# Five chunks of up to 496 tokens in place of eight of 288 in a feed-forward stage, with its weights in six groups

## The chip, the cores and the metric

The kernel runs on one core of a Trainium2 chip. The metric is the device time of one execution in microseconds; the times below are medians of several executions. The core has a matrix engine (TensorE, PE in the profile; its weight loads are PEld), VectorE (DVE), ScalarE (ACT) and GpSimd (POOL), which run side by side and wait for each other by semaphores, and 16 DMA engines, whose queue is fed here by SyncE (SP). Operands lie in SBUF, 128 partitions wide; TensorE writes to PSUM, which has eight banks of 512 f32 columns.

## The reference, cut to what matters

Three layers follow each other, on 4 x 576 = 2304 tokens of 512 features. The second one is the stage that is changed: 2048 hidden features, in 16 blocks of 128.

```python
def reference(q, k, v, s, U, V, w_ch1, w_ch2, w_gate, wq, wk, wv, wo):
    x = attention(q, k, v, s)            # causal, with a bias from cumulated gates; 4 x 8 heads of 64
    u = x + (U @ V mixed over the tokens of a batch)(x)
    x = u + np.maximum(u @ w_ch1, 0.0) @ w_ch2       # feed-forward, 512 -> 2048 -> 512
    return gated_attention_experts(x, w_gate, wq, wk, wv, wo)   # 4 experts, the best two of each token
```

The result has to be that of f32. TensorE is used in a faster mode with fewer bits of the operands, so each f32 operand a is split into a high part ah and the rest al, and a product is made of three: ah bh + ah bl + al bh. The weights arrive as 64-bit floats and are turned into f32 on the chip.

## The kernel before

**Stages.** The program has three stages. In the first (0 to 309 us) the 32 heads of attention run, and in their gaps the mixing of batches 0 to 2 and the first three hidden blocks (FA = 3) of these batches, whose results go to DRAM (aD). The second (309 to 673 us) is the feed-forward stage with the other 13 blocks, L790 to L916. The third holds the experts' attention and the output.

**Tiling of the feed-forward stage.** The tokens lie along the columns, and a chunk has CH = 288 of them, so there are eight chunks. The 13 blocks are taken in groups, `GROUPS = [2, 3, 3, 3, 2]`. A group goes over all chunks, every second group backwards, so that the chunk at a turn is used twice; this list of pairs (group, chunk) is `items`. In group 0 the chunks of the last batch (two of the eight) are preceded by the first three blocks on them, since the first stage did not do these. The unit of work is a slot, one block f on one chunk c. In it `ffn1` (L818) issues 12 matmuls (four pieces of 128 features, three products each) into one of three PSUM banks, from the parts uh and ul of the chunk and the block's weights; ScalarE then writes hh, the high part of the result after relu (L830), and VectorE hl, the low part (L831). `ffn2` (L837) of a pair (f, c) comes two slots later (`len(pend) > 2`): 12 matmuls into four accumulators (facc), 128 output features each. After the last block of a group VectorE adds the four accumulators to aT, in the last group to uT (L851).

**What runs beside it.** Each slot also issues background work, after its matmuls:
- `uprep` makes uh and ul of the next chunk out of uT (`u_split`, L273): four copies on ScalarE (uh, L277) and four subtractions (ul, L278), the first on VectorE, the other three on GpSimd (ULF = "vggg"). In a group of three blocks two of the four come in each of the first two slots, in a group of two all four in the first slot. Two sets of tiles (`fua`, `fub`) take turns.
- `conv` makes the weights of the next group: four pieces of 256 columns to a block. A piece is loaded (c_raw), ScalarE squares it (c_mk, L106), VectorE takes six instructions (L109, L113, L118, L122, L127, L131), ScalarE writes wh (L198) and GpSimd wl (L201). The steps of neighbouring pieces are interleaved (PLAIN), and they are spread over the slots of a group from the third on: at slot sl so many are issued that (issued) x (nsl - 3) is no less than (sl - 3) x nconv.
- `wp_tasks` loads and splits the weights of the last stage (wpr to WPh on ScalarE and WPl on VectorE, L766), eight pieces, one step at each chunk from the second chunk of group 2 on.
- `mixq`, in group 0, is the mixing of the last batch, two tasks to a slot; its row blocks are split into xh and xl (L241).
- `g_x2` splits the first batch for the last stage (XH, XL) in the last slots.

**What sets the order.** This stage and the one before are issued in the order in which the program writes them, engine by engine (`manual_schedule`, closed at L918): what stands behind a waiting instruction on the same engine waits too. After that line a scheduler orders the last stage. The lines that the change touches or the steps of the prediction use are CH and GROUPS (L27, L47), `u_split`, `ffn_tasks`, `uprep`, `ffn1`, `ffn2`, the loop over `items` from L868, and the pools of weights (`w01p`, `wts`), of u and of the last stage's x2 and y.

## Time and profile before

| | us |
|---|---|
| median of 3 executions (lowest, highest) | 876.32 (875.93, 877.03) |
| the profiled execution | 875.31 |
| its span in the trace | 873.1 |
| TensorE busy in the span | 817.1 (94%) |
| VectorE busy | 602.3 (69%) |
| ScalarE busy | 467.6 (54%) |
| GpSimd busy | 308.1 (35%) |

The span reaches from the first instruction to the last of one execution; the execution's own time has 2.2 us more, and it lies 1.0 us under the median. TensorE's mean granted clock over the span is 0.988 of the full one. The trace names each instruction by engine, line and tile; a busy time is the union of its durations. A matmul's duration reaches from its start to its modelled end and so overlaps the next one; what a row of matmuls takes is read from their starts. The idle time before an instruction is put down to the event that ended it.

### The profile page before, as it was taken

The page shows a single profiled execution, that of the slowest core. Times are in us where ns is not written, and L with a number is a line of the kernel's source. Part 1 is how long each engine was busy: PE and PEld are TensorE (multiplying, and loading weights), DVE is VectorE, ACT ScalarE, POOL GpSimd, SP SyncE. Part 2 cuts the span into 40 slices and gives each one's busy share as a digit, 9 for nine tenths or more (in the row PEclk, how much of TensorE's full clock was granted, in tenths as well). Part 3 has the DMA queues.
Part 4 walks back from the last instruction along what each step waited for, and adds up shares of the span by engine and source line. Part 5 has one row for each costly group of instructions (what it writes and reads, how often), then busy time and mean ns, then how long its engine had stood idle before and what let it go on. Part 6 is the DMA issues. An engine that isn't in the chain of part 4 may idle for free.

```text
span 873.1 us, 17681 instructions
## 1 busy us (share of the span) xinstructions
PE 817.1 (94%) x6104; PEld 750.8 (86%) x6104; DVE 602.3 (69%) x1755; ACT 467.6 (54%) x1382; POOL 308.1 (35%) x458
## 2 busy tenths in 40 slices
PE   3787888999999999999999999999999999999998
PEld 3665676898987789999999999999999989899875
DVE  7787888877787249986875887576546675656541
ACT  6686678866677343323432443333243476566673
POOL 4445254544344224322432432232233033221241
PEclk9997899999999999999999999999999999999999
DMA  7888568787560151120121221121000121211221
GB/s 205 227 230 201 135 179 230 176 208 202 151 180 17 55 187 37 50 61 25 50 53 34 61 61 42 46 62 38 1 1 2 41 43 30 64 46 38 60 69 55
DMA packets 36945, 79.66 MB, mean 91 GB/s; under 512 B 4792, under 2 KB 7992, under 8 KB 36856
## 3 DMA queue, kind: packets, MB, share of 16 engines
q1 hardware_dynamic: 36856, 78.53, 33.8%
q8 instruction: 49, 0.80, 0.4%
q14 instruction: 40, 0.33, 0.1%
HBM read 38.80 MB, written 8.40 MB: 54 GB/s over the span
## 4 chain that ended last, share of the span: by engine, by line
PE 74%; DVE 11%; ACT 5%; DMA 4%; issue 4%; POOL 1%; SPq 1%; DVEq 0%; ACTq 0%; POOLq 0%
PE facc L844 17%; PE hps L826 17%; PE pv L432 9%; PE qkp L1034 6%; PE t L403 4%; PE vps L971 3%; PE ops L1057 3%; PE facc L308 3%; PE qk L362 3%; PE qk L363 3%; PE hps L294 2%; PE t L406 2%; DVE P L373 2%; DMA c_raw_w<-in_w_dram 1%; ACT P L380 1%
## 5 line engine op out<-in xcount | busy, mean ns | idle before, releaser
L278 POOL TENSOR_TENSOR ul<-uT,uh 128x288 fp32r<-128x288 f32 x126 | 103.6, 840 | 176.1 <-ACT uh L277 161.4
L380 ACT ACTIVATE P<-P,stat 64x64 f32<-64x64 f32 (+4 forms) x240 | 133.8, 558 | 46.4 <-DVE stat L373 42.8
L373 DVE CUSTOM_DVE_ANT_0 P<-qk,mask 64x64 f32<-64x64 f32 (+4 forms) x240 | 116.6, 487 | 46.3 <-PE qk L363 30.2
L391 POOL TENSOR_SCALAR P<-P,stat 64x64 f32<-64x64 f32 (+4 forms) x160 | 101.5, 648 | 133.0 <-DVE stat L386 87.2
L362 PE MATMUL qk<-R,L 128*128 128x288 f32 (+4 forms) x288 | 96.6, 340 | 23.1 <-DVE L L573 10.9
L830 ACT ACTIVATE hh<-hps 128x288 fp32r<-128x288 f32 x110 | 44.8, 407 | 135.5 <-PE hps L826 135.4
L844 PE MATMUL facc<-hh,wh 128*128 128x288 f32 x376 | 111.4, 296 | 0.7 <-DVE aT L851 0.7
L76 ACT ACTIVATE pt<-t 64x64 f32<-64x64 f32 (+5 forms) x304 | 89.8, 335 | 41.5 <-PE t L406 35.3
L826 PE MATMUL hps<-ul,wh 128*128 128x288 f32 x376 | 111.3, 296 | 0.0
L826 PE MATMUL hps<-uh,wl 128*128 128x288 f32 x376 | 111.3, 296 | 0.0
L826 PE MATMUL hps<-uh,wh 128*128 128x288 f32 x376 | 111.1, 295 | 0.0
L844 PE MATMUL facc<-hh,wl 128*128 128x288 f32 x376 | 111.0, 295 | 0.0
L844 PE MATMUL facc<-hl,wh 128*128 128x288 f32 x376 | 110.9, 295 | 0.0
L831 DVE SCALAR_TENSOR_TENSOR hl<-hps,hh 128x288 fp32r<-128x288 f32 x110 | 50.1, 456 | 87.6 <-ACT hh L830 87.3
L403 PE MATMUL t<-ident,P 128*128 128x128 f32 x480 | 89.4, 285 | 16.1 <-ACT pt L76 5.3
L391 POOL TENSOR_SCALAR P<-P,stat,pt 64x64 f32<-64x64 f32 (+4 forms) x80 | 48.2, 615 | 127.8 <-DVE stat L386 35.6
L363 PE MATMUL qk<-R,L 68*128 68x288 f32 (+9 forms) x288 | 89.6, 316 | 1.2 <-DMA L<-Cd 0.8
L362 PEld LDWEIGHTS qk<-R,L 128*128 128x128 f32 x288 | 57.5, 200 | 31.5 <-issue 15.0
L403 PEld LDWEIGHTS t<-ident,P 128*128 128x128 f32 x480 | 58.6, 143 | 29.5 <-issue 16.9
L432 PE MATMUL pv<-pt,V 128*64 128x288 f32 (+4 forms) x768 | 79.2, 355 | 0.5 <-DVE stat L373 0.3
L432 PEld LDWEIGHTS pv<-pt,V 128*64 128x64 f32 x768 | 52.5, 144 | 27.5 <-issue 7.0
L201 POOL TENSOR_TENSOR wl<-c_a_w,wh 128x256 fp32r<-128x256 f32 x56 | 43.3, 774 | 91.3 <-ACT wh L198 88.7
(177 smaller groups left out, 2204.3 us busy)
## 6 DMA issues: line engine op xcount, KB each, us to landing
c_raw_w<-in_w_dram SPq DMA_DIRECT2D x64, 256.0 KB
uT<-in_qk_dram SPq DMA_DIRECT2D x15, 576.0 KB
L<-HI SPq DMA_DIRECT2D x28, 288.0 KB
R<-HI SPq DMA_DIRECT2D x28, 288.0 KB
V<-in_v_dram SPq DMA_DIRECT2D x16, 320.0 KB
R<-uT SPq DMA_DIRECT2D x14, 288.0 KB
L<-uT SPq DMA_DIRECT2D x14, 288.0 KB
aD<-stage SPq DMA_DIRECT2D x6, 576.0 KB
```

The source lines that it names most:

```text
L76: nc.scalar.activation(out=out, in_=in_, func=AF.Copy)
L278: eng.tensor_tensor(out=l_, in0=src, in1=h_.bitcast(F32), op=OP.subtract)
L362: nc.tensor.matmul(ps[:, bk, :w], lhsT=q1[:, rows], rhs=k1[:, c0:c0 + w], start=True, stop=False)
L363: nc.tensor.matmul(ps[:, bk, :w], lhsT=q2[:, rows], rhs=k2[:, c0:c0 + w], start=False, stop=True)
L373: nc.vector.tensor_tensor_reduce(out=po, in0=view, in1=mk, scale=-1.0, scalar=3.0e38, op0=OP.add, op1=OP.min, accum_out=stat[P - M:, 0, t: ...
L380: nc.scalar.activation(out=po, in_=po, func=AF.Exp, scale=-1.0, bias=stat[P - M:, 0, t:t + 1], accum_out=stat[P - M:, 1, t:t + 1])
L391: nc.gpsimd.tensor_scalar(out=pv, in0=pv, scalar1=stat[r0:, 2, t:t + 1], scalar2=1.0 if gate is None else gate(t)[r0:], op0=OP.mult, op1=O ...
L403: nc.tensor.transpose(ps[:, P * kb:P * kb + P], Pn[:, c0:c0 + P], ident)
L432: nc.tensor.matmul(ps[64 * hh:64 * hh + 64, half, lo - a:e - a], lhsT=V(hh)[:, kb, :], rhs=pt[:, PST * kb + lo:PST * kb + e], start=kb == ...
L826: nc.tensor.matmul(ps, lhsT=w[:, 0, cs], rhs=x, start=i == 0, stop=i == 11)
L844: nc.tensor.matmul(accs[c][d], lhsT=w[:, 1, cs], rhs=x, start=f == fs[0] and i == 0, stop=f == fs[-1] and i == 2)
L1034: nc.tensor.matmul(ps[:, :HALF], lhsT=wsl(w, "qk", k, col, col + P), rhs=xx[:, c0:c0 + HALF], start=i == 0, stop=i == 11)
```

## The change

- Chunks: four of CW = 496 tokens and one of 320 (CN, C0) in place of eight of 288, in the second stage alone. CH stays for the work that the first stage does.
- Groups: [2, 2, 3, 2, 2, 2] in place of [2, 3, 3, 3, 2]; the groups with index 1 and 3 go backwards (BACK). Where two groups follow each other in the same direction, 4 and 5 behind 3 among them, u of the first chunk is made again.
- The first three blocks in group 0 take only tokens of the last batch (`first_of`): 256 columns of the fourth chunk and the whole fifth.
- Memory: a single tile, `keep`, is allocated once. It holds the weights of the first three blocks and later of groups 2 and 4 (`w_keep`), one set of u (`u_keep`) and the hidden parts in the first stage, and in the last stage x2 (XS), y (ys) and two operands (l1s). The other set of u is the tile `ub`. The weights of groups 1, 3 and 5 come from a pool of two (`w_pool`).
- Background: the four parts of u come two to a slot in every group; mixing comes up to four tasks to a slot, two behind the first product and two behind the second; conversions are spread from the second slot on (nsl - 2 in place of nsl - 3); the weights of the last stage are split from the second chunk of group 1 on, in place of group 2; x2 of the first batch is split in the last two chunks.

```diff
 CH = 288
-NCH = TOK // CH
+CW = 496
+CN = [CW, CW, CW, CW, TOK - 4 * CW]
+C0 = [0, CW, 2 * CW, 3 * CW, 4 * CW]
+NCH = len(CN)
...
-GROUPS = [2, 3, 3, 3, 2]
+GROUPS = [2, 2, 3, 2, 2, 2]
+BACK = (1, 3)
...
-                    Wh[f] = wpool().tile([P, 2, DM], F32R, tag="wh", name=f"wh_{f}")
-                    Wl[f] = wpool().tile([P, 2, DM], F32R, tag="wl", name=f"wl_{f}")
+                    Wh[f], Wl[f] = place(f)
...
+    keep = ctx.enter_context(tc.tile_pool(name="keep", bufs=1, side="right")).tile([P, FA * 4 * DM + 14 * CH], F32R,
+                                                                                name="keep")
+    UB = FA * 4 * DM
+
+    def w_keep(f):
+        i = (f if f < FA else f - FA - sum(GROUPS[:2]) if f < FA + sum(GROUPS[:3]) else f - FA - sum(GROUPS[:4]))
+        return (keep[:, (2 * i + x) * 2 * DM:(2 * i + x + 1) * 2 * DM].rearrange("p (x c) -> p x c", x=2)
+                for x in range(2))
...
+    def u_keep(k, w):
+        return (keep[:, UB + (2 * k + x) * w:UB + (2 * k + x + 1) * w] for x in range(2))
...
+    XS = {0: [keep[:, x * KD * S:(x + 1) * KD * S].rearrange("p (k j) -> p k j", k=KD) for x in range(2)]}
+    ys = [[keep[:, UB + (2 * pr + x) * S:UB + (2 * pr + x + 1) * S] for x in range(2)] for pr in range(2)]
+    l1s = [keep[:, c:c + 2 * S + 64] for c in (2 * KD * S, UB + 4 * S)]
...
-        wts = [cx.enter_context(tc.tile_pool(name="f_w0", bufs=3))]
+        w0 = cx.enter_context(tc.tile_pool(name="f_w0", bufs=2))
...
-        fub = cx.enter_context(tc.tile_pool(name="f_u", bufs=1))
+        ub = cx.enter_context(tc.tile_pool(name="f_u", bufs=1)).tile([P, 8, CW], F32R, name="ub")
...
-        fu = [fua, fub]
+        fu = [u_keep, lambda k, w: (ub[:, 2 * k + x, :] for x in range(2))]
...
+        def w_pool(f):
+            return [w0.tile([P, 2, DM], F32R, tag=f"w{n}", name=f"w{n}_{f}") for n in "hl"]
+
+        def first_of(fs, c):
+
+            return max(0, TOK - S - C0[c]) if fs[0] < FA else 0
...
-                if gi == 2 and l[0][1] != c and not WP:
                     mxs.close()
-                    w01.close()
-                    fus.close()
-                    fu[fu.index(fua)] = cx.enter_context(tc.tile_pool(name="f_u2", bufs=1))
                     wpp = wg.enter_context(tc.tile_pool(name="wpp", bufs=1, side="right"))
...
-                    ffn1(f, c, hi, lo)
+                    ffn1(f, c, hi, lo, first_of(fs, c))
+                    for _ in range(2):
+                        if mixq:
+                            mixq.pop(0)()
                     pend.append((f, c, fs))
                     if len(pend) > 2:
                         ffn2(*pend.pop(0))
+                    for _ in range(2):
+                        if mixq:
+                            mixq.pop(0)()
...
-                    for _ in range(2 if len(fs) > 2 else KD):
+                    for _ in range(2):
                         if uq:
                             uq.pop(0)()
...
-                    if gi == len(items) - 1 and c >= NCH - 3 and len(x2.get(0, "  ")[0]) < KD:
+                    if gi == len(items) - 1 and c >= NCH - 2 and len(x2.get(0, "  ")[0]) < KD:
                         g_x2(0, len(x2[0][0]) if 0 in x2 else 0)
-                    while conv and (nconv - len(conv)) * (nsl - 3) < (sl - 3) * nconv:
+                    while conv and (nconv - len(conv)) * (nsl - 2) < (sl - 2) * nconv:
                         conv.pop(0)()
```

On VectorE, in group 1 before, while three blocks are converted (c_h, c_a, c_z are steps of a piece, hl_1_7 is the low part of block 7 on chunk 1, aT the sums, the first row here the last of four):

```order
L851 TENSOR_TENSOR aT_4003<-facc_5_2_3_5910,aT_4003 128x288
L113 TENSOR_SCALAR c_a_w10_256_6020<-c_h_w10_256_5973 128x256
L118 SCALAR_TENSOR_TENSOR c_a_w10_256_6020<-c_h_w10_256_5973,c_a_w10_256_6020 128x256
L122 TENSOR_SCALAR c_z_w10_256_6023<-c_a_w10_256_6020 128x256
L127 SCALAR_TENSOR_TENSOR c_h_w10_256_5973<-c_raw_w10_256_5886,c_z_w10_256_6023 128x256
L131 TENSOR_TENSOR c_a_w10_256_6020<-c_h_w10_256_5973,c_a_w10_256_6020 128x256
L831 SCALAR_TENSOR_TENSOR hl_1_7_6045<-hps_1_7_6031,hh_1_7_6044 128x288
L109 SCALAR_TENSOR_TENSOR c_h_w10_512_6064<-c_mk_w10_512_6025,c_raw_w10_512_5971 128x256
L113 TENSOR_SCALAR c_a_w10_512_6068<-c_h_w10_512_6064 128x256
L831 SCALAR_TENSOR_TENSOR hl_0_5_6084<-hps_0_5_6070,hh_0_5_6083 128x288
```

And in group 1 of the change, where three blocks are converted too, behind the four sums of the short chunk (WPl is a piece of the last stage's weights):

```order
L880 TENSOR_TENSOR aT_3907<-facc_5_4_3_4787,aT_3907 128x320
L122 SCALAR_TENSOR_TENSOR c_a_w7_256_4827<-c_h_w7_256_4823,c_a_w7_256_4827 128x256
L126 TENSOR_SCALAR c_z_w7_256_4867<-c_a_w7_256_4827 128x256
L131 SCALAR_TENSOR_TENSOR c_h_w7_256_4823<-c_raw_w7_256_4808,c_z_w7_256_4867 128x256
L135 TENSOR_TENSOR c_a_w7_256_4827<-c_h_w7_256_4823,c_a_w7_256_4827 128x256
L113 SCALAR_TENSOR_TENSOR c_h_w7_512_4875<-c_mk_w7_512_4869,c_raw_w7_512_4821 128x256
L117 TENSOR_SCALAR c_a_w7_512_4879<-c_h_w7_512_4875 128x256
L122 SCALAR_TENSOR_TENSOR c_a_w7_512_4879<-c_h_w7_512_4875,c_a_w7_512_4879 128x256
L126 TENSOR_SCALAR c_z_w7_512_4882<-c_a_w7_512_4879 128x256
L131 SCALAR_TENSOR_TENSOR c_h_w7_512_4875<-c_raw_w7_512_4821,c_z_w7_512_4882 128x256
L135 TENSOR_TENSOR c_a_w7_512_4879<-c_h_w7_512_4875,c_a_w7_512_4879 128x256
L780 TENSOR_TENSOR WPl_4764<-wpr_0_4765,WPh_4763 128x514
```

Where five conversion instructions stood between the sums and hl_1_7 and two before hl_0_5, ten and a WPl now stand between the sums and hl_2_5, the next row.

On ScalarE, in the same group before (hh_1_6 is the high part of block 6 on chunk 1, uh_0_2 a part of chunk 0, which is the next one, wh a piece of new weights, c_mk the square):

```order
L830 ACTIVATE hh_1_5_5945<-hps_1_5_5932 128x288
L277 ACTIVATE uh_0_0_5961<-uT_68 128x288
L277 ACTIVATE uh_0_1_5965<-uT_68 128x288
L198 ACTIVATE wh_10_5975<-c_a_w10_0_5925 128x256
L830 ACTIVATE hh_1_6_5992<-hps_1_6_5979 128x288
L277 ACTIVATE uh_0_2_6012<-uT_68 128x288
L277 ACTIVATE uh_0_3_6016<-uT_68 128x288
L106 ACTIVATE c_mk_w10_512_6025<-c_raw_w10_512_5971 128x256
L830 ACTIVATE hh_1_7_6044<-hps_1_7_6031 128x288
L198 ACTIVATE wh_10_5975<-c_a_w10_256_6020 128x256
```

And in the change (`ub` and `keep` hold u and the new weights; x2 stands for two copies):

```order
L857 ACTIVATE hh_2_5_4905<-hps_2_5_4892 128x496
L286 ACTIVATE ub_3920<-uT_68 128x496 x2
L201 ACTIVATE keep_74<-c_a_w7_512_4879 128x256
L110 ACTIVATE c_mk_w8_0_4938<-c_raw_w8_0_4888 128x256
L201 ACTIVATE keep_74<-c_a_w7_768_4933 128x256
L857 ACTIVATE hh_2_6_4964<-hps_2_6_4951 128x496
L286 ACTIVATE ub_3920<-uT_68 128x496 x2
L110 ACTIVATE c_mk_w8_256_4990<-c_raw_w8_256_4942 128x256
L201 ACTIVATE keep_74<-c_a_w8_0_4948 128x256
```

The second pair of u copies, which was followed by a whole slot of block 7 before the next chunk began, is now issued in the chunk's last slot, behind two pieces wh of the weights that wait for VectorE.

## Rows read from the trace of the kernel before

**Rows 1.** the page: busy time, share of the span, instructions, by engine:
```profile
PE 817.1 (94%) x6104; PEld 750.8 (86%) x6104; DVE 602.3 (69%) x1755; ACT 467.6 (54%) x1382; POOL 308.1 (35%) x458
```

**Rows 2.** stretches: length; busy us of PE, PEld, DVE, ACT, POOL; clock; DMA:
```profile
309.00:364.00 55.00, 52.34 (x382) 50.34 (x383) 44.28 (x99) 22.33 (x60) 19.74 (x24) 1.00 0.31 104
350.00:360.00 10.00, 8.83 (x67) 8.60 (x65) 9.60 (x22) 3.83 (x11) 4.20 (x5) 1.00 0.16 50
404.00:481.00 77.00, 77.00 (x582) 77.00 (x581) 57.41 (x137) 28.83 (x79) 26.08 (x34) 1.00 0.18 46
```

**Rows 3.** TensorE's timeline around 500 us: start, duration, line, operation, out<-in, shapes:
```profile
500.45 0.30 PE L826 MATMUL hps<-uh,wh 128*128 128x288 f32 x1
...
502.97 0.29 PE L844 MATMUL facc<-hl,wh 128*128 128x288 f32 x1
```

**Rows 4.** TensorE's timeline near the end of the program:
```profile
864.05 0.39 PE L1057 MATMUL ops<-WPh,yh 128*128 128x512 f32 x1
...
868.64 0.40 PE L1057 MATMUL ops<-WPh,yl 128*64 128x512 f32 x1
```

**Rows 5.** VectorE's timeline, 420 to 425 us:
```profile
420.62 1.06 DVE L118 SCALAR_TENSOR_TENSOR c_a_w<-c_h_w,c_a_w 128x256 uint32<-128x256 uint32 x1
...
422.04 0.43 DVE L127 SCALAR_TENSOR_TENSOR c_h_w<-c_raw_w,c_z_w 128x256 f32<-128x256 uint32 x1
...
422.99 0.46 DVE L831 SCALAR_TENSOR_TENSOR hl<-hps,hh 128x288 fp32r<-128x288 f32 x1
423.36 1.54 DVE L851 TENSOR_TENSOR aT<-facc,aT 128x288 f32<-128x288 f32 x4
```

**Rows 6.** VectorE by line, 328-361 us: count, busy, mean ns, idle before:
```profile
L127 DVE SCALAR_TENSOR_TENSOR c_h_w<-c_raw_w,c_z_w 128x256 f32<-128x256 uint32 x6 | 3.5, 587 | 0.2
L122 DVE TENSOR_SCALAR c_z_w<-c_a_w 128x256 uint32<-128x256 uint32 x6 | 3.4, 561 | 0.2
L118 DVE SCALAR_TENSOR_TENSOR c_a_w<-c_h_w,c_a_w 128x256 uint32<-128x256 uint32 x5 | 3.2, 640 | 0.1
L113 DVE TENSOR_SCALAR c_a_w<-c_h_w 128x256 uint32<-128x256 uint32 x5 | 2.6, 512 | 0.2
L109 DVE SCALAR_TENSOR_TENSOR c_h_w<-c_mk_w,c_raw_w 128x256 f32<-128x256 f32 x6 | 2.6, 426 | 0.4
L131 DVE TENSOR_TENSOR c_a_w<-c_h_w,c_a_w 128x256 f32<-128x256 f32 x6 | 2.5, 423 | 0.2
```

**Rows 7.** GpSimd's timeline, with the idle time before and what ended it:
```profile
420.59 0.81 POOL L278 TENSOR_TENSOR ul<-uT,uh 128x288 fp32r<-128x288 f32 x1 [1.13 <-ACT uh L277]
```

**Rows 8.** VectorE by line and shape, 364 to 672 us:
```profile
L851 DVE TENSOR_TENSOR aT<-facc,aT 128x288 f32<-128x288 f32 x104 | 40.1, 448 | 0.0
...
L278 DVE TENSOR_TENSOR ul<-uT,uh 128x288 fp32r<-128x288 f32 x29 | 13.6, 467 | 0.0
...
L766 DVE TENSOR_TENSOR WPl<-wpr,WPh 128x514 fp32r<-128x514 f32 x8 | 5.8, 721 | 5.5 <-ACT WPh L765 5.5
```

**Rows 9.** VectorE by line and shape, 300 to 364 us:
```profile
L241 DVE TENSOR_TENSOR xl<-mx,xh 128x512 fp32r<-128x512 f32 x4 | 2.7, 690 | 1.7 <-ACT xh L76 1.7
```

**Rows 10.** timeline of ScalarE, VectorE and TensorE, 353 to 358 us:
```profile
353.06 0.40 ACT L830 ACTIVATE hh<-hps 128x288 fp32r<-128x288 f32 x1
...
356.49 0.45 DVE L831 SCALAR_TENSOR_TENSOR hl<-hps,hh 128x288 fp32r<-128x288 f32 x1
...
357.36 0.40 PE L844 MATMUL facc<-hh,L 128*128 128x288 f32 x1 [1.17 <-DVE aT L851]
```

**Rows 11.** ScalarE's waits, 364-672 us: total us, times, longest:
```profile
ACT wh L198 <- DVE c_a_w L131: 38.4, 25, 3.1
ACT c_mk_w L106 <- DMA c_raw_w<-in_w_dram: 20.9, 14, 2.5
```

**Rows 12.** GpSimd by line and shape, 364 to 672 us:
```profile
L278 POOL TENSOR_TENSOR ul<-uT,uh 128x288 fp32r<-128x288 f32 x87 | 71.3, 838 | 125.3 <-ACT uh L277 110.7 <-PE facc L844 11.7 <-PE hps L826 2.8
L201 POOL TENSOR_TENSOR wl<-c_a_w,wh 128x256 fp32r<-128x256 f32 x38 | 29.2, 769 | 75.2 <-ACT wh L198 75.2
```

84 lines of the change are left out of this document (41 added, 43 removed).

## The prediction

> **What bounds the kernel now.** I read the engines' totals first: TensorE is busy 94% of the span, VectorE 69% [rows 1]. A total says little, so the table by stretch came next. While a group of three weight columns runs (404 to 481 us), TensorE is busy all 77.0 us and VectorE 57.4 us; in the first 55 us of the feed-forward stage TensorE loses 2.7 us [rows 2]. So the stage is bound by TensorE, and VectorE has about a quarter of its time left. The start times in TensorE's own timeline then give the step from one matmul to the next, which is what a stream costs (the durations overlap): 19 steps of 288 columns take 2.52 us, 132.6 ns each [rows 3], and 20 steps of 512 columns take 4.59 us, 229.5 ns each [rows 4]. At the full 2.4 GHz, which the granted clock of 1.00 in this stage means, 288 columns are 120 ns and 512 are 213 ns; 12.6 and 16.2 ns come on top. Last I read VectorE's rows by form, and where they are late.
>
> **What the change gives on TensorE.** A slot is one hidden block f on one chunk: 12 matmuls of the first product and 12 of the second. Before there are 13 x 8 slots plus 3 x 2 for the first three blocks on the last batch: 110 x 24 = 2640 matmuls of 288 columns, 2640 x 132.6 ns = 350.1 us. After there are 13 x 4 x 24 = 1248 of 496 columns, 312 + 72 = 384 of 320 and 72 of 256: 1704 in all, over the same number of columns. A straight line through the two steps (0.433 ns a column and 8.0 ns fixed) gives 222.6, 146.4 and 118.8 ns, so 277.8 + 56.2 + 8.6 = 342.6 us. **The gain is 7.5 us.** Bounds: 936 matmuls less at 12.6 ns each, were all of the excess fixed, 11.8 us; and 5 us, if both steps are read wrong by half a nanosecond the wrong way. I take 7.5, from the row at 512, which is near 496.
>
> The rows put the fixed part at 8 to 13 ns. By the Trainium skill, "TensorE: Matmul & The Clock Gate", section "Back-to-back issue gap", a warm matmul costs its columns at 2.4 GHz plus about 2.5 ns; by that, 936 fewer matmuls would give 2.3 us. The rows disagree with it (132.6 against 122.5 ns at 288 columns), and the sum goes by the rows.
>
> **What it costs on VectorE.** The weights are converted on VectorE in pieces of six instructions, four pieces to a block, while the group before computes. VectorE's 57.4 us in the stretch of rows 2 hold 24 hl, 32 adds, 8 ul and 72 instructions of 12 pieces. In a row of such instructions one takes 0.37 to 0.385 us (four adds 1.54 us, hl to add 0.37 us [rows 5]); 64 x 0.375 = 24.0 us, which leaves 33.4 us, 2.8 us a piece. Where VectorE is never idle (350 to 360 us, 9.6 of 10 us busy [rows 2]) a piece is dearer: its six means are 0.587, 0.561, 0.640, 0.512, 0.426 and 0.423 us, 3.15 together [rows 6]. The reason can be seen: GpSimd's ul runs from 420.59 for 0.81 us [rows 7], and the VectorE instruction that starts at 420.62 takes 1.06 us instead of 0.43 [rows 5].
>
> Five chunks make the group short. A group of two blocks is now 8 slots of 24 x 222.6 ns = 5.34 us and 2 of 3.51 us: 49.7 us, and in group 1 the 12 pieces of the next group (three blocks) must fit there, where before they had 24 slots of 3.18 us, 76.4 us. They start after the second slot, so within eight slots, 42.7 us. Wider instructions grow by 1.08 ns a column (448 ns at 288 [rows 8], 690 ns at 512 [rows 9]), by 0.225 us at 496 and 0.035 us at 320. VectorE's work in those eight slots:
> - 12 pieces: 33.4 us (calm) to 37.8 us (never idle)
> - 8 hl of 0.60 us: 4.8 us
> - adds: 3 chunks x 4 x 0.61 and one short chunk x 4 x 0.42: 9.0 us
> - 3 ul of 0.69 us (0.467 [rows 8] + 0.225): 2.1 us
> - 2 splits of the last layer's weights, which move from group 2 to group 1, 0.72 us each [rows 8]: 1.4 us
>
> That is 50.7 to 55.1 us against 42.7: VectorE ends 8.0 to 12.4 us late. I take 11, near the row where it is never idle. How much is free? In the stretch of before where it was late, an hl began at 356.49, its hh had ended at 353.06 + 0.40 us: 3.0 us late; TensorE lost 1.17 us [rows 10]. So 1.9 us was free at slots of 3.18 us, about 3 us at 5.34. **Group 1 costs 8 us.** Lower bound 5 (8.0 late). Upper bound 12: ScalarE's queue is tied to VectorE's, since wh waits for the piece (25 waits, 38.4 us [rows 11]), and hh and the copies uh stand behind it. Before, a group of two copied all four parts of the next chunk in its first slot; now parts 2 and 3 come in the last. After the first product of that slot come hh and two uh (0.4 us each at 288 [rows 10], some 0.6 at 496) and two ul on GpSimd (838 ns at 288 and 769 at 256 [rows 12], so 1.29 us at 496): 4.4 us. TensorE wants the last of them after 12 + 10 matmuls, 4.9 us. Only 0.5 us is free there, and lateness beyond it is a loss in each chunk.
>
> Groups 3 and 4 (two pieces to a block and slot pair) are near balance: in a chunk of 10.68 us VectorE has 2 pieces (5.6 to 6.3), hl 1.2, adds 2.44, ul 0.69 and some 0.36 for the moved splits: 10.3 to 11.0 us. In the short chunk that ends group 4 two slots last 7.0 us and hold 9.5 us or more. Nothing (all absorbed) to 8 us; I take 4.
>
> **What I cost at nothing.** Group 0 converts 8 pieces instead of 12, so the 1.17 us goes, and the last batch's mixing runs with four tasks a slot instead of two; its row blocks then wait for PSUM banks until hl and xl are done, some 2 to 3 us by hand, about what 309 to 364 us lost before [rows 2]: 0, from -2 to +2. Loads of the last layer's weights stand earlier in SP's queue between the raw weight loads; ScalarE waits for those anyway (14 waits, 20.9 us [rows 11]), and a later one counts within the bounds of group 1. The single tile changes which memory is shared, not what waits for what: in the order of the changed kernel each first product waits for its own uh and ul as before, and the last stage's matmuls stand in the same order. GpSimd's ul gain a third in all but have room (26.1 of 77 us busy [rows 2]).
>
> **Sum.** -7.5 + 8 + 4 + 0 = +4.5 us on a span of 873.1 us: 877.6. With 2.2 us around the span the profiled execution took 875.3 us, 1.0 below the median of 876.3; so 881 us for a median.
>
> **The rivals.**
> - VectorE's lateness is absorbed (not slower). Its place is group 1, its price the 2.8 us of a calm piece: 8.0 us late, 3 to 5 us lost, nothing in groups 3 and 4: -7.5 + 3 = 872 us. It decides at a piece of about 3.0 us, where loss and gain meet. For it: the mean over the calm stretch. Against: a queue that never empties meets GpSimd's work in each piece. 22%.
> - Break-even: group 1 alone loses, and 7 to 8 us: 876 us. 10%.
> - ScalarE's queue passes the lateness on to the u copies: 12 in group 1 and 7 to 8 in groups 3 and 4, so +12: 888 us. For it: 0.5 us of room; against it: TensorE's loss slows what VectorE is asked for. 15%.
> - The fixed cost of a matmul is 2.5 ns, and the gain 2.3 us instead of 7.5: 881 + 5 = 886 us. Two steps of the trace speak against it. (This is the skill's rule above.) 3%.
>
> **How the numbers follow.** The forecast, VectorE late in groups 1, 3 and 4, holds 50%, its own range 878.5 to 887. Slower is 50 + 15 + 3 = 68%, no change (within 0.2%, 1.8 us, about what a measurement of this kernel can tell) 10%, faster 22%. The range reaches down through the first rival to 870 and up to 889; below and above I leave some 8% each (both bounds at their best would give 867, at their worst 893).
>
> **What would show it.** Step of 496-column matmuls 222 to 223 ns: the gain is right. VectorE over 95% busy in group 1, TensorE idle 5 to 12 us there, ended by ul on GpSimd, uh on ScalarE or aT on VectorE: the cost is right. TensorE above 97% busy through group 1 would make the prediction wrong, as would pieces under 2.9 us there, or a last stage that starts with other waits.

## The result, and the profile after

The changed kernel takes 887.1 us (median of 4, 885.9 to 887.8), the kernel before 876.7 us (4 runs, 875.9 to 877.9): a ratio of 1.012, with a 95% interval of 1.0103 to 1.0136. It is slower, as forecast, and within the range (870 to 889), but by 10.5 us where the sum said 4.5.

The profiled execution took 887.7 us with a span of 885.9 us, 12.8 us over the span of before. That is more than the 10.5 us between the medians, since the profiled execution lies 0.6 us above its median here and lay 1.4 us below it before. By the first and last matmul of the feed-forward stage that splits into 3.0 us before the stage (its first matmul starts at 312.0 instead of 309.0 us), 9.7 us in it (to 685.5 instead of 672.8 us) and 0.1 us behind it. First come the totals, which answer to [rows 1]:

```profile
PE 818.3 (92%) x5168; PEld 699.7 (79%) x5168; DVE 612.0 (69%) x1666; ACT 462.7 (52%) x1303; POOL 316.4 (36%) x428
```

As before, they show little: TensorE is busy about as long as it was, in a span that is 12.8 us longer. The table by stretch (columns as in [rows 2]), here of groups 0, 1 and 2, shows where the time goes:

```profile
312.00:388.80 76.80, 75.09 (x416) 65.42 (x417) 50.44 (x104) 24.28 (x55) 19.67 (x19) 1.00 0.25 81
388.80:452.10 63.30, 54.62 (x254) 44.64 (x253) 51.70 (x103) 23.30 (x51) 24.00 (x23) 0.97 0.20 55
452.20:528.40 76.20, 76.20 (x349) 64.62 (x350) 51.19 (x99) 22.91 (x50) 20.89 (x21) 0.98 0.13 35
```

Group 1, in which three blocks are converted, has 8.7 us in which TensorE does nothing, and a clock below the full one; group 2 has none. For more than that the starts of all matmuls of the stage were taken from TensorE's timeline: each step from one matmul to the next, less its undisturbed time, is put to the group whose block the later of the two works on, and their sum is called the group's loss below. (In group 0 it holds the mixing's matmuls too, so only differences count there. The second products of a group's last two blocks are issued in the next group's first slots and count for their own group.) The undisturbed step comes from the same rows, here of group 2:

```profile
491.55 0.39 PE L873 MATMUL facc<-hh,keep 128*128 128x496 f32 x1
...
494.04 0.39 PE L873 MATMUL facc<-hh,keep 128*128 128x496 f32 x1
```

Eleven steps take 2.49 us; over all 1248 matmuls of 496 columns, waits left out, the mean is 225.05 ns, and 146.9 at 320 columns, 118.6 at 256 and, before, 132.9 at 288. The terms of the sum then measure as follows.

| us | forecast | measured |
|---|---|---|
| matmuls (350.9 to 345.8) | -7.5 | -5.1 |
| group 1 | +8 | +13.8 |
| groups 3 and 4 (and 5) | +4 | +1.4 + 0.0 + 1.3 |
| group 0 (loss 12.8 to 10.9), "at nothing" | 0 | -1.9 |
| start of the stage (not named) | 0 | +3.0 |
| last stage | 0 | +0.1 |
| sum | +4.5 | +12.6 |

For group 1 (395 to 460 us) TensorE waits for these (us in total, times, longest):

```profile
PE facc L873 <- DVE aT L880: 2.8, 1, 2.8
PE hps L853 <- ACT ub L286: 2.2, 1, 2.2
PE hps L853 <- POOL keep L287: 2.1, 4, 1.1
PE hps L853 <- POOL ub L287: 1.0, 1, 1.0
PE hps L853 <- ACT keep L286: 0.5, 1, 0.5
```

Four of the five are parts of u, on ScalarE or GpSimd. What ScalarE waits for in the same group answers to [rows 11]:

```profile
ACT keep L201 <- DVE c_a_w L135: 14.6, 7, 2.9
ACT c_mk_w L110 <- DMA c_raw_w<-in_w_dram: 8.5, 6, 2.4
...
ACT c_mk_w L110 <- DVE c_h_w L131: 4.5, 2, 2.2
ACT c_mk_w L110 <- DVE c_h_w L113: 3.0, 2, 1.6
```

And the timeline of VectorE, ScalarE, TensorE and GpSimd at TensorE's wait of 2.2 us:

```profile
415.39 1.50 DVE L113 SCALAR_TENSOR_TENSOR c_h_w<-c_mk_w,c_raw_w 128x256 f32<-128x256 f32 x1
...
418.93 0.42 DVE L135 TENSOR_TENSOR c_a_w<-c_h_w,c_a_w 128x256 f32<-128x256 f32 x1
...
419.38 0.42 ACT L201 ACTIVATE keep<-c_a_w 128x256 fp32r<-128x256 f32 x1 [1.97 <-DVE c_a_w L135]
419.71 0.57 ACT L857 ACTIVATE hh<-hps 128x496 fp32r<-128x496 f32 x1
420.17 1.11 ACT L286 ACTIVATE ub<-uT 128x496 fp32r<-128x496 f32 x2
420.83 0.49 PE L853 MATMUL hps<-ub,wh 128*128 128x496 f32 x1 [2.22 <-ACT ub L286]
420.86 2.68 POOL L287 TENSOR_TENSOR ub<-uT,ub 128x496 fp32r<-128x496 f32 x2 [0.25 <-ACT ub L286]
```

VectorE ends a piece at 419.35, ScalarE has stood 1.97 us before its wh, and only then come hh and the two copies of u that TensorE has waited for since 418.6. The first piece's L113 took 1.50 instead of 0.43 us while GpSimd worked, as in [rows 5, 7]. Behind such a wait comes a second price, the clock:

```profile
418.40:422.40 4.00, 0.74 (x3) 0.22 (x2) 3.70 (x9) 2.34 (x5) 2.27 (x3) 0.93 0.21 66
422.40:425.30 2.90, 2.90 (x7) 2.25 (x8) 2.77 (x6) 0.02 (x1) 1.14 (x1) 0.51 0.00 0
425.40:427.50 2.10, 2.10 (x11) 1.77 (x10) 1.89 (x5) 0.29 (x1) 0.74 (x1) 1.00 0.49 129
```

TensorE was busy 0.74 of 4.0 us, then was granted 0.51 of the clock (1.2 GHz, the lower of its two levels) for 2.9 us, and the full one (2.4 GHz) behind that. The same happens at 452 us, behind the wait of 2.8 us. Some twelve matmuls of group 1 start 0.41 us apart instead of 0.225, which is 2.2 of the 13.8 us.

### The profile page after: what moved, and what is told of

Read it like the earlier page. It is cut to its first block, busy times and chain, and to the rows that moved or that the text cites. A ratio compares the mean times of both kernels' runs of the same rounds, so it can differ in the third digit from the quotient of the medians.

```text
span 885.9 us, 15510 instructions
## 1 busy us (share of the span) xinstructions
PE 818.3 (92%) x5168; PEld 699.7 (79%) x5168; DVE 612.0 (69%) x1666; ACT 462.7 (52%) x1303; POOL 316.4 (36%) x428
## 4 chain that ended last, share of the span: by engine, by line
PE 69%; DVE 11%; ACT 5%; issue 5%; DMA 5%; POOL 3%; SPq 1%; DVEq 0%; ACTq 0%; POOLq 0%
PE facc L873 16%; PE hps L853 16%; PE pv L443 8%; PE qkp L1060 6%; PE t L414 4%; PE vps L997 3%; PE facc L319 3%; PE ops L1083 3%; PE qk L373 3%; PE qk L374 3%; PE hps L306 2%; PE t L417 2%; DMA L<-Cd 1%; DMA c_raw_w<-in_w_dram 1%; DVE P L384 1%
## 5 line engine op out<-in xcount | busy, mean ns | idle before, releaser
L384 DVE CUSTOM_DVE_ANT_0 P<-qk,mask 64x64 f32<-64x64 f32 (+4 forms) x240 | 116.5, 486 | 45.2 <-PE qk L374 24.6
L858 DVE SCALAR_TENSOR_TENSOR hl<-hps,hh 128x496 fp32r<-128x496 f32 (+2 forms) x71 | 44.1, 621 | 94.4 <-ACT hh L857 94.3
L287 POOL TENSOR_TENSOR keep<-uT,keep 128x496 fp32r<-128x496 f32 (+2 forms) x57 | 61.0, 1085 | 96.7 <-ACT keep L286 96.5
L373 PE MATMUL qk<-R,L 128*128 128x64 f32 (+2 forms) x192 | 67.9, 358 | 23.2 <-DVE L L586 10.9
L287 POOL TENSOR_TENSOR ub<-uT,ub 128x496 fp32r<-128x496 f32 (+1 forms) x39 | 49.5, 1283 | 69.1 <-ACT ub L286 67.2
L873 PE MATMUL facc<-hh,keep 128*128 128x496 f32 (+2 forms) x248 | 72.4, 357 | 0.0
L417 PE MATMUL t<-ident,P 128*64 128x128 f32 x240 | 59.1, 279 | 1.9 <-ACT pt L80 1.8
L374 PEld LDWEIGHTS qk<-R,L 68*128 68x128 f32 (+1 forms) x288 | 57.5, 200 | 2.4 <-DMA R<-Cd 0.6
L880 DVE TENSOR_TENSOR aT<-facc,aT 128x496 f32<-128x496 f32 (+1 forms) x100 | 57.1, 627 | 0.0
L873 PEld LDWEIGHTS facc<-hh,keep 128*128 128x128 f32 x248 | 45.0, 188 | 6.0
L873 PE MATMUL facc<-hh,wh 128*128 128x496 f32 (+1 forms) x120 | 45.6, 380 | 2.9 <-DVE aT L880 2.8
```

The lines of the kernel that those rows point to most:

```text
L287: eng.tensor_tensor(out=l_, in0=src, in1=h_.bitcast(F32), op=OP.subtract)
L373: nc.tensor.matmul(ps[:, bk, :w], lhsT=q1[:, rows], rhs=k1[:, c0:c0 + w], start=True, stop=False)
L374: nc.tensor.matmul(ps[:, bk, :w], lhsT=q2[:, rows], rhs=k2[:, c0:c0 + w], start=False, stop=True)
L384: nc.vector.tensor_tensor_reduce(out=po, in0=view, in1=mk, scale=-1.0, scalar=3.0e38, op0=OP.add, op1=OP.min, accum_out=stat[P - M:, 0, t: ...
L417: nc.tensor.transpose(ps[0:64, x:x + P], Pn[:, c0:c0 + 64], ident)
L873: nc.tensor.matmul(accs[c][d][:, :n], lhsT=w[:, 1, cs], rhs=x, start=f == fs[0] and i == 0, stop=f == fs[-1] and i == 2)
```

## The experiments

All are edits of the changed kernel, timed against the kernel before on the same chip (875.4 to 876.2 us there). The loss of each group, in us, from the one trace of each kernel:

| kernel | time | ratio (95%) | 0 | 1 | 2 | 3 | 4 | 5 |
|---|---|---|---|---|---|---|---|---|
| changed | 887.1 | 1.0103-1.0136 | 10.9 | 13.8 | 0.1 | 1.4 | 0.0 | 1.3 |
| e1_copies | 896.9 | 1.0213-1.0248 | 9.7 | 18.6 | 0.8 | 2.8 | 4.8 | 0.2 |
| e2_spread | 889.9 | 1.0137-1.0167 | 15.5 | 12.1 | 0.1 | 2.2 | 0.0 | 0.1 |
| e3_five | 884.6 | 1.0055-1.0106 | 10.9 | 10.6 | 0.1 | 1.5 | 0.0 | 1.3 |
| e4_raw3 | 882.8 | 1.0055-1.0085 | 10.9 | 9.0 | 0.1 | 1.5 | 0.0 | 1.3 |
| e6_stream | 887.8 | 1.0111-1.0162 | 10.9 | 15.5 | 0.1 | 1.6 | 0.3 | 0.2 |
| e7_both | 880.4 | 1.0037-1.0072 | 10.9 | 8.9 | 0.0 | 1.5 | 0.2 | 0.2 |
| e8_carry | 885.9 | 1.0088-1.0147 | 10.9 | 5.0 | 6.2 | 2.5 | 1.6 | 0.8 |
| e9_all | 880.2 | 1.0033-1.0065 | 10.9 | 7.3 | 0.6 | 1.2 | 0.4 | 0.7 |
| e10_early | 892.3 | 1.0157-1.0219 | 9.7 | 16.4 | 0.6 | 2.3 | 0.2 | 3.0 |
| e11_none | 873.4 | 0.9966-0.9992 | 10.9 | 0.2 | 0.0 | 1.4 | 0.0 | 1.3 |
| e12_raw3five | 877.1 | 1.0004-1.0032 | 10.9 | 4.0 | 0.0 | 1.4 | 0.0 | 1.2 |
| e13_carry_early | 881.9 | 1.0062-1.0092 | 9.7 | 6.3 | 2.3 | 1.5 | 1.3 | 1.9 |
| e14_ulv | 889.9 | 1.0124-1.0187 | 12.2 | 11.2 | 0.1 | 2.8 | 2.3 | 3.3 |
| e15_wpcarry | 877.7 | 1.0004-1.0039 | 10.9 | 3.4 | 1.4 | 1.8 | 0.1 | 0.8 |
| e16_wpcarryulv | 882.8 | 1.0045-1.0101 | 12.2 | 4.6 | 0.1 | 2.4 | 2.8 | 2.4 |
| e18_thin | 875.4 | 0.9981-1.0014 | 9.7 | 0.5 | 4.3 | 0.5 | 0.0 | 1.2 |
| e19_three | 873.4 | 0.9966-0.9993 | 9.8 | 1.2 | 1.9 | 0.5 | 0.0 | 1.2 |

### What in the twelve pieces costs

The first theory was that of the third rival: VectorE is late, and ScalarE's queue hands this on to the copies of u. Four first edits (e1_copies, e2_spread, e3_five and e4_raw3) took one suspect each; e11_none took the pieces away.

**e4_raw3**, a third raw buffer:

```diff
-        raw = pool.tile([P, width], I64, tag="c_raw", name=f"c_raw_{name}", bufs=2)[:m, :n]
+        raw = pool.tile([P, width], I64, tag="c_raw", name=f"c_raw_{name}", bufs=RAWS[0])[:m, :n]
...
+        RAWS[0] = 3
```

> The changed kernel with three buffers for the raw weight pieces in the feed-forward stage instead of two, so that a load can start one piece earlier. Rival C (the loads' latency sets the pace of the pieces and so of ScalarE's queue): group 1 loses 4 to 7 us less, 880 to 883 us. Theory (VectorE's load, passed on by ScalarE): within 1 us of the changed kernel, 886 to 888 us; the waits for the loads turn into waits for VectorE.

It took 882.8 us, what rival C said: group 1 lost 9.0 us. The loads have gone from ScalarE's waits there:

```profile
ACT keep L202 <- DVE c_a_w L136: 20.6, 9, 3.7
ACT c_mk_w L111 <- DVE c_h_w L114: 4.2, 2, 2.8
ACT hh L858 <- PE hps L854: 2.9, 1, 2.9
```

So a third buffer gives 4.8 of the 13.8 us back. Some 2.2 of these are the clock: the waits that are left are shorter, and no matmul of the group runs at half the clock any more:

```profile
395.50:448.00 52.50, 47.12 (x211) 37.61 (x211) 46.12 (x93) 21.14 (x47) 22.54 (x21) 1.00 0.21 61
```

With two buffers a load can start only when the piece before the last has been read by L131: one ends at 424.78 us and the next load is issued at 424.85. VectorE itself did not wait for a load in the changed kernel (no L113 stands idle for c_mk); ScalarE's queue hands the lateness on. The square c_mk waits for the load, and hh behind it is late, and so are hl and the sums, for which TensorE then waits 2.8 us until 452.1:

```profile
449.78 0.43 ACT L110 ACTIVATE c_mk_w<-c_raw_w 128x256 f32<-128x256 f32 x1 [2.44 <-DMA c_raw_w<-in_w_dram]
450.11 0.56 ACT L857 ACTIVATE hh<-hps 128x496 fp32r<-128x496 f32 x1
450.71 0.68 DVE L858 SCALAR_TENSOR_TENSOR hl<-hps,hh 128x496 fp32r<-128x496 f32 x1 [1.62 <-ACT hh L857]
```

In the kernel before the same wait stood in its group 1, and TensorE lost nothing there (ScalarE's wait, then the stretch of the group):

```profile
ACT c_mk_w L106 <- DMA c_raw_w<-in_w_dram: 6.3, 6, 2.1
...
388.80:465.40 76.60, 76.60 (x578) 76.60 (x577) 58.73 (x142) 28.28 (x76) 25.87 (x33) 1.00 0.18 46
```

There twelve pieces were spread over 21 slots of 3.18 us, one in 5.6 us; here over eight slots, 42.7 us by the slot times forecast, one in 3.6 us.

**e3_five**, one VectorE instruction of six (the one that puts sign and top exponent bit back) left out in group 1:

```diff
     def v1():
+        if LESS[0]:
+            return
...
+            LESS[0] = gi == 1
```

> The changed kernel without one of the six VectorE instructions of each of the twelve pieces converted in group 1 (the one that puts sign and top exponent bit back, so the third group's weights come out wrong). It takes 11 x 0.494 / 11 x 12 = 5.9 us off VectorE in group 1, and nothing else. Theory and rival A: group 1 loses 5 to 8 us instead of 13.8, 879 to 882 us. Rival B (the copies' place alone): 886 to 888 us. If the latency of the raw loads (rival C, ScalarE waits 8.5 us for them in group 1) sets the pace: 885 to 887 us.

It took 884.6 us: a gain of 2.5 us, 3.2 in group 1, half of what was expected and in between the theories. **e12_raw3five** has both edits:

> The changed kernel with three raw buffers and, in group 1, five VectorE instructions a piece instead of six (the third group's weights come out wrong). Three buffers alone left 9.0 us in group 1, five instructions alone 10.6. If the two causes are apart (late loads, and VectorE's work): group 1 loses 4 to 6 us, 877.5 to 880 us. If both only loosen the same wait: 8 to 9 us, 882 to 883 us.

It took 877.1 us, and group 1 lost 4.0 us. With the loads out of the way 5.9 us less on VectorE give 5.0 us back. So the late loads and VectorE's work are two causes, but they do not simply add: one by one the edits give 4.8 and 3.2 us, together 9.8, since each hides a part of the other. The buffer is worth 4.8 us with six instructions and 6.6 with five. What the last 4.0 us are was not taken apart.

**e11_none** converts nothing in group 1; the third group takes what lies in its place:

```diff
+            if gi == 1:
+                conv = []
+                for f in nx:
+                    Wh[f], Wl[f] = w_keep(f)
```

> The changed kernel without the conversions in group 1: the third group computes with the weights that lie in its place from before, and twelve pieces with their loads, ScalarE, VectorE and GpSimd work are left out. If the twelve pieces are the whole cause in group 1: it loses 1.5 us or less, as group 5, which converts nothing, and the time is 874 to 876 us. If the wide chunks cost something by themselves there (four wider sums between two chunks, with one set of accumulators): 4 us or more stay, 878 us or more.

It took 873.4 us, and group 1 lost 0.2 us:

```profile
395.60:437.20 41.60, 41.60 (x194) 35.04 (x193) 17.90 (x32) 12.07 (x23) 13.87 (x11) 1.00 0.09 26
```

TensorE is busy throughout. Wide chunks, wide sums and two copies in a slot cost nothing there without the pieces. The twelve pieces, with their loads and their work on three engines, are the whole of group 1's loss.

### Where the copies of u stand

**e1_copies** and **e10_early** move them. In e1_copies all four stand in the chunk's first slot:

```diff
-                    for _ in range(2):
+                    for _ in range(2 if len(fs) > 2 else KD):
                         if uq:
                             uq.pop(0)()
```

> The changed kernel, with all four parts of the next chunk's u split in the first slot of a group of two, as the kernel before did. Group 1 of the changed kernel loses 13.8 us, of which 8.8 us stand in front of the first product's matmuls for parts 2 and 3 of u. Theory: VectorE is late with the weight pieces, and ScalarE, which waits for it with wh, passes this on to the two copies of u in the last slot; without them behind it only VectorE's own lateness is left, 5 to 8 us in group 1, and 879 to 882 us in all. Rival A: the loss is VectorE's load alone and shows in another wait: 886 to 888 us. Rival B: the last slot is too short for two copies and two subtractions, whatever VectorE does: group 1 loses 1 us or less, 874 to 875 us.

It took 896.9 us, worse than each of the three theories had it. TensorE's waits in group 1 moved to the sums (aT), which stand behind hl and the pieces on VectorE:

```profile
PE facc L873 <- DVE aT L880: 10.7, 4, 4.3
PE hps L853 <- POOL ub L287: 1.0, 3, 0.5
```

In e10_early the last two copies stand ahead of the second slot's first product:

```diff
+                    if j == 1:
+                        for _ in range(2):
+                            if uq:
+                                uq.pop(0)()
                     ffn1(f, c, hi, lo, first_of(fs, c))
...
-                    for _ in range(2):
+                    for _ in range(2 if j == 0 else 0):
```

> The changed kernel with the last two copies of u of each chunk issued ahead of the second slot's first product, so that they stand ahead of its hh on ScalarE and nothing else moves. In group 1, 8.8 of 13.8 us stand before the matmuls that read these parts, in groups 3 and 5 all of 1.4 and 1.3 us. If their place is the cause: group 1 loses 5 us, groups 3 and 5 nearly nothing, 876 to 878 us. If VectorE is late with the pieces (its work and what GpSimd blocks) and the raw loads add to it: group 1 loses what it did, only at other waits, and 2 us come from groups 3 and 5: 884 to 886 us.

It took 892.3 us, more than either theory had it, with 16.4 us lost in group 1. The copies' place is therefore not the cause in the dense group; they only stand where the lateness shows. Elsewhere the early place helps in part: group 0 lost 1.2 us less in both, but groups 3 to 5 together lost 5.1 us more in e1_copies (4.8 of it in group 4) and 2.8 more in e10_early. Why the dense group became worse than it was, **e14_ulv** was to tell, with three raw buffers and all ul on VectorE:

```diff
-                h_, l_ = u_split(*(x[:, :CN[c]] for x in place(k, CW)), C0[c], k,
-                                 nc.vector if ULF[k] == "v" else nc.gpsimd)
+                h_, l_ = u_split(*(x[:, :CN[c]] for x in place(k, CW)), C0[c], k, nc.vector)
```

> The kernel with three raw buffers (882.8 us, group 1 loses 9.0), and all four ul of a chunk on VectorE instead of one there and three on GpSimd. If GpSimd's ul hold up VectorE's conversion steps (three of 1.34 us a chunk, against three of 0.67 us on VectorE): up to 2 us a chunk come off VectorE, group 1 loses 4 to 6 us, 878 to 880 us. If only VectorE's own work counts: 2 us a chunk come on top, group 1 loses 12 to 15 us, and groups 3 to 5 lose too, 888 us or more.

It took 889.9 us, as VectorE's own work had it, 7.1 more than with three buffers alone, and lost more in every group but group 2. TensorE now waits for VectorE's ul over the stage:

```profile
PE hps L853 <- DVE ub L288: 8.1, 8, 3.4
PE hps L853 <- DVE keep L288: 4.2, 7, 1.4
```

VectorE's instructions do take longer beside GpSimd's subtractions (the L113 above), but in VectorE's own queue the subtractions are dearer here. Some 2 of the 4.8 us that e1_copies lost more in group 1 are the clock: 24 matmuls start 0.41 us apart there, behind longer waits. Why the waits of e1_copies and e10_early grew stays open.

### Order and spread of the pieces

**e6_stream** takes the other interleaving of a piece's steps (STREAM, in which wh follows the next piece's first step), **e7_both** that and three raw buffers:

```diff
-                                   PLAIN))
+                                   STREAM))
```

> The changed kernel with another interleaving of the conversion's steps in the feed-forward stage (STREAM in place of PLAIN, both in the source): wh and wl of a piece are issued behind the first VectorE step of the next piece, not right behind the piece's own last step. New theory, after four runs: ScalarE's queue sets the pace. It waits in group 1 of the changed kernel 14.6 us with wh for the sum just issued on VectorE and 8.5 us with c_mk for raw loads, and hh and the copies of u stand behind; whole pieces now come back to back. Then group 1 loses 7 to 10 us instead of 13.8: 881 to 884 us. If VectorE's load in group 1 is what costs: its work is the same, 886 to 888 us.

> The changed kernel with that interleaving and with three raw buffers, which alone brought group 1 from 13.8 to 9.0 us lost. New theory (ScalarE's waits for pieces): both waits gone, group 1 loses 3 to 5 us, 876 to 879 us. VectorE's load: as with three raw buffers alone, 882 to 883 us.

They took 887.8 us, no gain, and 880.4 us, with the group 1 of three buffers alone (8.9 against 9.0). The theory that ScalarE's waits for wh set the pace said 881 to 884 and 876 to 879. But the edit did not take these waits away. In group 1 of e6_stream their sum is what it was (388 to 450 us):

```profile
ACT keep L201 <- DVE c_a_w L135: 14.6, 7, 3.3
```

So the two runs show that this order of the steps gains nothing, and not that the waits cost nothing. **e2_spread** starts each group's conversions in its first slot:

```diff
-                    while conv and (nconv - len(conv)) * (nsl - 2) < (sl - 2) * nconv:
+                    while conv and (nconv - len(conv)) * nsl < sl * nconv:
```

> The changed kernel, with the conversions of each group spread from its first slot on instead of the third. In group 1 twelve pieces then have ten slots (49.7 us by the slot times forecast) instead of eight (42.7 us). Theory and rival A (VectorE's load): 7 us more room, group 1 loses 5 to 7 us instead of 13.8, 879 to 881 us in all. Rival B (the last slot too short for the copies): no gain, 886 to 888 us, since the copies stay where they are.

It took 889.9 us, above both theories: group 0, where the pieces now meet the mixing, lost 4.6 us more, and group 1 only 1.7 less, not the 7 to 9 of VectorE's load. With two raw buffers, twelve pieces in ten slots cost nearly as much as in eight. **e8_carry** carries conversions over into the group that uses them, and **e9_all** joins it with e7_both, **e13_carry_early** that with the early copies:

```diff
+CARRY = 3
...
-                    while conv and (nconv - len(conv)) * (nsl - 2) < (sl - 2) * nconv:
+                    for _ in range(-(-nleft // CARRY)):
+                        if left:
+                            left.pop(0)()
+                    while conv and (nconv - len(conv)) * (nsl - 2 + CARRY) < (sl - 2) * nconv:
                         conv.pop(0)()
-            for f in conv:
-                f()
+            left += conv
```

> The changed kernel with each group's conversions spread over three more slots, into the group that uses them (a piece is still issued ahead of the first matmul that reads it). In group 1 then 8/11 of twelve pieces are converted, 8.7. VectorE's load: 3.3 pieces of 2.8 to 3.15 us less in group 1, 9 to 10 us, so group 1 loses 4 us or less and little comes in group 2: 876 to 878 us. New theory (ScalarE waits for each piece that comes close behind another): the loss falls with the number of pieces, 13.8 x 8.7 / 12 = 10 us, 882 to 884 us.

> The changed kernel with all three: three raw buffers, the other interleaving, and the conversions carried over into the next group. Both theories: group 1 loses 1 us or less, groups 3 and 5 as much as before (1.4 and 1.3 us); 887.1 - 13 = 873 to 875 us, some 2 us under the kernel before.

> The kernel with three raw buffers, the other interleaving and the carried conversions (880.2 us), and the last two copies of u ahead of the second slot's first product. In its group 1 VectorE is busy 45.4 of 49 us; TensorE loses 7.3 us there, 3.5 of them before the matmuls that read the late copies. If VectorE is what is late: group 1 loses 5 to 7 us, 878 to 880 us. If the copies' place is: 3 us or less, 874 to 877 us.

In e8_carry group 1 lost 8.8 us less, as VectorE's load says, but group 2 lost 6.2, since pieces came late there (one wait of 3.0 us for wh among them): 885.9 us, above both theories. e9_all took 880.2 us, some 6 more than both theories had it; its group 1 still lost 7.3. e13_carry_early took 881.9 us, above both again; its group 1 lost 6.3, as lateness on VectorE says, and group 2 2.3.

**e15_wpcarry** has three raw buffers, the carried conversions, and the last stage's weights split from group 2 on (two steps a chunk there), as in the kernel before:

```diff
-                if gi == 1 and l[0][1] != c and not WP:
+                if gi == 2 and l[0][1] != c and not WP:
```

> The kernel with three raw buffers, conversions carried over into the next group by three slots, and the last stage's weights split from group 2 on as in the kernel before, two steps a chunk there. VectorE's work in group 1 falls by 3.3 pieces (9 us) and two WPl (1.5 us), and group 2 takes them. If work on VectorE is what is left after the loads: group 1 loses 2 to 4 us, 876 to 878 us. If not: 880 us or more, as with the carried conversions before.

It took 877.7 us, as the theory of VectorE's work had it: group 1 lost 3.4. Against e9_all (7.3) two things differ, the interleaving, which made 0.1 us in group 1 with three buffers, and the last stage's weights. If the interleaving is as neutral with carried pieces, the two splits that the change had moved into group 1 (1.5 us of VectorE's time) cost some 3.9 us there, and 0.8 in group 2 where they stand now. **e16_wpcarryulv** is that kernel with ul on VectorE, as in e14_ulv:

> The kernel just described with all ul on VectorE as well. If GpSimd's ul hold up VectorE for longer than its own ul would take: 874 to 876 us, about the kernel before. If not: 4 us or more above it.

It took 882.8 us, 5.2 more, again with losses in groups 0, 3, 4 and 5. **e18_thin**, made from e15_wpcarry, spreads group 1's twelve pieces over thirteen slots, **e19_three** over twelve, and both put all copies of u in the first slot in groups 0 and 5 alone:

```diff
-            nleft = len(left)
+            nleft, lag, carry = len(left), (2, 1, 4, 2, 2, 2)[gi], CARRY if gi == 1 else 0
...
-                    for _ in range(2):
+                    for _ in range(KD if gi in (0, len(items) - 1) else 2):
...
-                    while conv and (nconv - len(conv)) * (nsl - 2 + CARRY) < (sl - 2) * nconv:
+                    while conv and (nconv - len(conv)) * (nsl - lag + carry) < (sl - lag) * nconv:
```

> The changed kernel with three raw buffers, group 1's conversions spread from its second slot to the fourth of group 2 (twelve pieces over thirteen slots), the last stage's weights split from group 2 on, and all four copies of u in the first slot in groups 0 and 5 alone, where few or no pieces are converted. From losses seen one by one: group 0 loses 9.7 us instead of 10.9 (mixing included), group 1 some 2.5, group 2 1, group 3 1.4, group 4 0, group 5 0.2, in all 14.8 against 18.4 of the best so far (877.7): 874 us, 2 us under the kernel before. If these gains don't add up: 876 to 878 us.

It took 875.4 us, no difference from before: group 1 lost 0.5, but a weight came late in group 2:

```profile
PE hps L855 <- ACT keep L203: 2.1, 1, 2.1
```

> The kernel just run with the carried pieces done one slot sooner: group 1's twelve pieces are spread over twelve slots, to the third of group 2, so that the first half of the third block's weights is issued two slots ahead of its first use. Group 1 lost 0.5 us and group 2 4.3, of which 2.1 was a wait for these weights and 1.6 the half clock behind it. If pieces per time are the cause: group 1 loses 0.5 to 1.5 us, group 2 0.5 or less: 872 to 873 us, 3 us under the kernel before. If a twelfth more density brings the loss back in group 1: 875 us or more.

It took 873.4 us, a ratio of 0.998 (0.9966 to 0.9993): 2 us under the kernel before and, by the two ratios, some 12 under the changed one, with every piece converted. In its group 1:

```profile
394.00:436.00 42.00, 41.25 (x191) 34.48 (x190) 40.01 (x75) 17.55 (x37) 19.94 (x19) 1.00 0.18 48
```

VectorE is busy 40.0 of 42.0 us, and TensorE 41.25. With VectorE 95% busy TensorE is idle 0.75 us here, at one piece a slot; the changed kernel issues twelve in eight slots. There VectorE was busy for 51.70 of 63.30 us, 82%, and TensorE idle for 8.7. So a high busy share of VectorE does not make the loss by itself. (e19_three also has the third buffer and the later splits, so the spacing of the pieces is not all that differs.)

**e17_384** keeps 12 pieces out of any short group by other means: six chunks of 384, groups [2, 3, 2, 2, 2, 2].

```diff
-CW = 496
+CW = 384
...
-GROUPS = [2, 2, 3, 2, 2, 2]
+GROUPS = [2, 3, 2, 2, 2, 2]
...
-        w0 = cx.enter_context(tc.tile_pool(name="f_w0", bufs=2))
+        w0 = cx.enter_context(tc.tile_pool(name="f_w0", bufs=3))
```

> The changed kernel with six chunks of 384 tokens, groups [2, 3, 2, 2, 2, 2] and three buffers in the pool of weights: the three blocks of group 1 are converted in group 0 (two blocks, 18 slots with the first three on the last batch), no group of two converts more than eight pieces. Matmuls: by the steps measured at 256 to 496 columns (5.0 + 0.444 ns a column) 1872 + 72 of 384 columns and 72 of 192: some 347 us, 3.5 less than before. If the pieces per time are what cost: groups 1 to 5 lose 1.5 us each or less, 874 to 878 us. If groups of two lose whatever they convert (copies in the last slot, sums twice as often): 880 us or more.

It took 882.8 us (0.76% over before, interval 0.51 to 1.02%), 880 or more, as the theory had it that groups of two lose whatever they convert, and not what the pieces per time said: group 1, with three blocks, lost 0.4 us, groups 2 to 4 2.5 to 3.2 us each, and group 5, which converts nothing, none, which speaks against that theory too. By the step measured at 384 columns (175.7 ns) a piece comes every 5.3 us in groups 2 to 4, nearly as rarely as in the kernel before. So the rate of the pieces is not the whole rule; in these groups TensorE waits for the sums and for the copies of u, and what would free them was not tried.

## Why the prediction was right in sign and wrong in size

- **What bounds the stage.** Right: TensorE, and VectorE with the pieces where the change makes a group short (e11_none and e12_raw3five).
- **The gain on TensorE.** Mis-sized, -5.1 instead of -7.5 us, at the bound of 5. I had drawn a line through 288 columns of this stage [rows 3] and 512 of the last one [rows 4], 0.433 ns a column and 8.0 ns fixed; the four widths in this stage lie on 0.444 and 5.0 ns, and 496 columns take 225.05 ns where 222.6 was forecast. The step would have shown "222 to 223 ns" to be right; it showed it wrong. By the Trainium skill, "TensorE: Matmul & The Clock Gate", section "Back-to-back issue gap", the fixed part is about 2.5 ns at full clock for a matmul by itself; for a stream with weight loads the section gives other figures. The trace of this stream lies between the 2.5 and my 8.0 ns, and its columns cost more than the 0.417 ns of 2.4 GHz. So the fourth rival's gain of 2.3 us was too low, as mine was too high.
- **Group 1.** The step that failed: 13.8 us where 8 was forecast, outside the bounds of 5 and 12, and 5.8 of the 8.1 us that the sum missed. The price of a piece on VectorE was right: the six instructions of a piece took 2.98 us in the mean (the forecast's ends were 2.8 and 3.15):

```profile
L117 DVE TENSOR_SCALAR c_a_w<-c_h_w 128x256 uint32<-128x256 uint32 x11 | 8.1, 740 | 0.9
L113 DVE SCALAR_TENSOR_TENSOR c_h_w<-c_mk_w,c_raw_w 128x256 f32<-128x256 f32 x11 | 6.7, 606 | 0.9
L122 DVE SCALAR_TENSOR_TENSOR c_a_w<-c_h_w,c_a_w 128x256 uint32<-128x256 uint32 x11 | 5.4, 494 | 0.3
L131 DVE SCALAR_TENSOR_TENSOR c_h_w<-c_raw_w,c_z_w 128x256 f32<-128x256 uint32 x10 | 4.3, 426 | 0.3
L135 DVE TENSOR_TENSOR c_a_w<-c_h_w,c_a_w 128x256 f32<-128x256 f32 x10 | 4.2, 425 | 0.3
L126 DVE TENSOR_SCALAR c_z_w<-c_a_w 128x256 uint32<-128x256 uint32 x11 | 3.2, 292 | 0.3
```

  Three raw buffers leave 9.0 us, so 8 was nearly right for the rest. What was put at nothing, with the words that a later load "counts within the bounds of group 1", were the raw loads: 4.8 us, of which some 2.2 are the half clock behind the long waits, a price that the sum did not have at all. The 14 waits of [rows 11] were free at one piece in 5.6 us. Issued at one in 3.6 us, the pieces came at one in 4.9 (their first steps on VectorE lie from 401.0 to 454.5 us), and ScalarE then stood before late loads with hh and u behind. The sign "VectorE over 95% busy in group 1" did not come, 82% of the group, but what it stood for did: from 400.2 to 449.1 us VectorE was busy for 44.67 of 48.90 us and idle in one piece for 0.6 us at most. The other sign came too: TensorE idle for 8.7 us, behind ul, uh and aT. The other misses partly cancel, by luck: +2.4 for the matmuls and +3.0 at the stage's start, -1.9 in group 0 and -1.3 in groups 3 to 5.
- **Groups 3 to 5.** They lost 2.7 us against 4. Most of it stands ahead of first products that wait for GpSimd's part of u, a wait that the forecast's balance of VectorE's work did not contain. Group 5 converts nothing; its 1.3 us stand at its first chunk, whose u is made in the last slots of group 4, beside group 4's last pieces. In e18_thin and e19_three, where group 5's own copies stand early, it still lost 1.2; in e2_spread and e6_stream, with the copies in their old place, 0.1 and 0.2. So the copies' place alone is not the cause, and how much of it is the 0.5 us of room that the third rival counted is not shown.
- **At nothing.** Group 0 gained 1.9 us, within the bounds given. The start of the stage, which the forecast did not name, lost 3.0 us. Of these 3.0 us, 1.35 are there already at 126 us, in the attention stage, where TensorE's order is the same; at that point the other kernels' traces, with the same first stage as the changed one, lie between -2.6 and +3.2 us of the kernel before, so this part varies from one execution to the next. The other 1.65 us lie at the hand-over, where the wider copies of the first chunk come in; that these are the reason is not shown. After, then before:

```profile
305.00:309.00 4.00, 3.72 (x21) 2.41 (x21) 0.68 (x2) 1.41 (x7) 2.12 (x2) 0.59 0.00 0
```

```profile
302.50:306.50 4.00, 3.50 (x31) 2.37 (x33) 0.68 (x2) 2.28 (x9) 1.79 (x3) 1.00 0.22 76
```

  The granted clock was 0.59 in this stretch after and 1.00 before. From one attention matmul near 285 us to the stage's first it took 24.3 us before, 26.0 here, 24.6 to 24.9 in twelve of the other traces and 25.6 to 26.0 in six: 0.3 to 0.6 us more is there in every trace, and some 1.1 on top of that in some executions.
- **The rivals.** The third one (ScalarE's queue passes the lateness on, 12 us in group 1) came nearest in size, and its waits are in the trace, but moving the copies of u (e1_copies and e10_early) made the time longer. Its path over ScalarE's queue can be read from the rows at 419 and 450 us, but what it hands on there is late loads as well as VectorE's work; no run takes ScalarE's waits away and leaves the pieces. The first one (absorbed) named a point of about 3.0 us a piece from which it would decide; at 2.98 the loss was full, and even without the late loads it was 9.0 us, so that point was put too high.
